# Raw weights to the place of their split parts, a third place for the chunks, x handed over by chunks of 128 tokens

## The chip, the cores and the metric
One core of one Trainium2 chip runs the whole kernel. It has five engines, each with an instruction queue that it works through in order: TensorE (PE, matmuls; PEld is its loading of weights), VectorE (DVE), ScalarE (ACT), GpSimd (POOL) and SyncE (SP), which here issues nearly all DMA transfers. The metric is the device time of one execution in microseconds.

## The reference
The input is four batches of 768 tokens with 8 heads of 48 elements. Three parts follow each other: a linear attention with a forget gate for each element, a layer of two matrices with a squared relu between them, and a soft mixture of experts.

```python
f = 1 / (1 + exp(-f_logit))
for t in range(S):                       # linear attention, per batch and head
    state = f[t][:, None] * state + outer(k[t], v[t])
    y[t] = q[t] @ state
x = y                                    # 3072 tokens x 384
h = maximum(x @ w_in, 0)                 # 384 -> 2048
x = (h * h) @ w_out                      # 2048 -> 384
logits = x @ phi                         # 32 slots: 8 experts, 4 slots each
d = softmax(logits, over tokens)
slot_out = per expert e: maximum((d.T @ x)[e] @ w1[e], 0) @ w2[e]
out = softmax(logits, over slots) @ slot_out
```

## The kernel before, in words
**Attention** runs in 24 chunks of 128 tokens, six to a batch. `chunk_load` (L129) brings a chunk's gate logits, k and q in one load `g<-fkq` (672 KB) into a place of pool g, and its v in another. `prep` (L145) works on them in place: exp of the logits (ACT L157), add 1 (DVE L161, on ACT for chunks 2 to 4), a running product along the tokens by four scans (DVE L163), a logarithm and an exp (ACT L170, L171), k times the product (DVE L172), and q times its inverse (DVE L178 to L180). The last of these, L180, is the last reader of the chunk's place. exp, add and scans are called the head of a chunk below. `knat`, `scores`, `state` and `values` do the matmuls; n is the transposed k copied out by ACT (L196). `values` writes minus y of a chunk into a tile y that holds a block of three chunks; after the third, six transfers (L269, L272) carry y of the whole block into x, the input of the layers (two of 216 KB, two of 48 and two of 24).

**The layers** run in 8 blocks of 384 tokens and 16 tiles of the inner dimension, 128 steps in all. A step (`layer1`, then `layer2`) has nine matmuls for `ph<-x,w`, on ACT a relu and two squares (`r` L347, `gh` L349, `r` L350), on DVE a subtraction (`gl<-r,gh`, L352), and nine matmuls for `o<-w,gh` and `o<-w,gl`. Each float32 product is done as three products of high and low parts, so x and w are split in two. The weights come as 64-bit floats: 16 raw tiles of 768 KB (`w_load`, L295, transfer L308), which `w_split` (L311) turns into a float32 `whi` with one ACT copy (L318), one ACT abs (L323) and three DVE instructions (L324, L325, L334), and `hl` (L114 on ACT, L115 on DVE) into a high and a low part in one of the 16 tiles of pool w. All 16 splits happen in the first 16 steps. The steps of blocks 0 and 1 are taken in turns (5, 9, 11 and 7 steps), from block 2 on block by block.

**Places.** Pool g has SLOTS = 4 places of 768 KB. Chunks 0, 1 and 2 take places 0, 1 and 2, and each later chunk takes places 0 and 1 in turn. Raw weights take places 2 and 3 in turn, each loaded one step ahead of its split. Two early loads of expert weights (`m2_load`, L516, transfer L527; in the steps 0 and 1 of block 3 in the order of the program) take places 2 and 3 after that, and when attention has ended, eight more loads take places 0 and 1 and six tiles of their own. In the last block's steps the loads go on into the 16 tiles of pool w as these come free, and what remains of the 32 loads stands at the end.

**The tail** (L536 on) runs the experts from these 32 tiles: `so<-m,ib` (L573) multiplies with the last of them; then the outputs.

**What sets the order.** The program is written as the loop of `fast_blocks`, with attention taken along by a table of targets. A scheduler then fixes the order of each engine's queue ahead of time, by its own model of times; on the chip an engine takes its queue in that order and waits where a semaphore isn't there yet. So where an instruction stands in a queue is fixed, and how long it waits is not.

Of the kernel before, what the change touches and what calls it, by code (L numbers as in the profile page):

```python
# [7 lines left out]
F32 = mybir.dt.float32  # L8
# [9 lines left out]
NP = H // 2  # L18
# [18 lines left out]
SLOTS = 4  # L37
PRE = 2
RAW = 6
AHEAD = 5  # L40
# [3 lines left out]
PREB = 3  # L44
# [14 lines left out]
class K:  # L59
# [70 lines left out]
    def chunk_load(self, i):  # L130
        nc, ap = self.nc, self.ap
        fkq = self.slot(i if i < 3 else (i + 1) % 2)[:DD].rearrange("d (x p t) -> d x p t", x=3, p=NP)
# [100 lines left out]
    def values(self, i):  # L233
# [18 lines left out]
        b, c = divmod(i, NC)  # L252
        if c == 0:
            self.y = ap.tile([DD, NP, TB], F32, tag="y", name="y", bufs=1)
        y = self.y
        t0 = c * C + before[0][0] * HC
        nc.scalar.mul(y[:, :, t0 : (c + 1) * C], pz[:, :, before[0][0] * HC :], -1.0)
        for j in range(2):
            o = y[:, :, c * C + j * HC : c * C + (j + 1) * HC]
            if U["S"][j] is None:  # L260
                nc.scalar.mul(o, py[j], -1.0)
            else:
                nc.vector.tensor_tensor(o, o, py[j], ALU.subtract)
        if c < NC - 1:
            return
        self.x_alloc(b)
        xl = self.x[b][1].bitcast(F32)
        for h in range(2):
            nc.sync.dma_start(out=xl[h * D : h * D + D], in_=y[h * HR : h * HR + D, :KT])  # L269
        for h in range(2):  # L270
            for e, n, kt, o in PLACE[6 + h]:
                nc.sync.dma_start(out=xl[o : o + n, kt], in_=y[h * HR + e : h * HR + e + n, KT])  # L272
# [26 lines left out]
    def w_load(self, ff):  # L299
        wide = self.A["w"].dtype != F32  # L300
        raw = self.slot(2 if ff > 1 and ff % 2 == 0 else 3)
# [9 lines left out]
    def w_split(self, ff, raw):  # L311

        nc, wr = self.nc, self.wr
        t = self.wp.tile([128, 2, 2 * DM], F32R, tag="w", name="w")
        if raw.dtype != F32:
# [3 lines left out]
            n = wr.tile([128, 2 * DM], I32, tag="whi", name="whi", bufs=2)  # L319
# [13 lines left out]
            raw = n.bitcast(F32)  # L333
            nc.vector.tensor_tensor(raw.bitcast(I32), n, lo, ALU.add)  # L334
        self.hl(t[:, 0], t[:, 1], raw)
# [181 lines left out]
    def m2_load(self):  # L517

        if self.loads < 32:
            j = self.loads % (SLOTS + RAW + NFF)  # L520
            if j < SLOTS:
                t = self.slot((j + 2) % SLOTS)
# [78 lines left out]
    def fast(self):  # L601
        with ExitStack() as main:
# [14 lines left out]
            raw = {0: self.w_load(0)}  # L617
# [4 lines left out]
    def fast_blocks(self, main, pst, ast, wst, raw):  # L622

        def stream():
            for i in range(2):
                yield from self.prep(i)
            for i in range(NCH):
# [3 lines left out]
                for j, n in enumerate((1, 1, 0, 0, 2) if ahead == 2 else (1, 1, 1, 0, 2)):  # L631
# [4 lines left out]
                    if j == (4 if i < 2 else 1) and i != 2 and new < NCH:  # L636
                        self.loaded[new] = self.chunk_load(new)
                    yield

# [39 lines left out]
        self.w_split(0, raw.pop(0))  # L679
# [219 lines left out]
```

## Time and profile before
| | us |
|---|---|
| median of three runs | 624.24 (623.1 to 625.67) |
| profiled execution, whole time | 626.73 |
| its span, first to last instruction | 624.9 |
| busy in it: PE, DVE, ACT | 585.5, 343.0, 335.5 |
| granted PE clock, mean | 0.986 of full speed |

The shares of the whole span (PE 94%, DVE 55%, ACT 54%) are an average of unlike stretches. In the first 41 us attention runs alone. Then the layers begin beside the rest of the splits of weights and attention at a high rate. From about 150 us layers and attention run side by side at a steady rate until 449 us, and then the layers alone until 573. The tail is last. What a microsecond is worth must be read in its own stretch, which the rows below allow.

### The profile page before, as it was taken

What the parts mean: (1) busy time and instruction counts of PE and PEld (TensorE: products, weight loads), DVE (VectorE), ACT (ScalarE), POOL (GpSimd) and SP (SyncE); (2) the same over time, 40 slices, a digit from 0 to 9 for tenths busy, and PEclk for the clock granted to TensorE, in tenths of its full rate; (3) what the DMA queues carried; (4) which work ended last, traced back from release to release, by engine and by line L of the source; (5) the groups of instructions that cost most, each with busy time, mean ns of one, the idle gap of its engine ahead of it and who ended that gap; (6) DMA issues with size and microseconds to landing.
All of it is one profiled execution on the core that took longest, in us unless ns stands there. A gap on an engine that the chain in (4) does not pass through costs nothing.

```text
span 624.9 us, 14327 instructions
## 1 busy us (share of the span) xinstructions
PE 585.5 (94%) x6065; PEld 525.3 (84%) x6065; DVE 343.0 (55%) x772; ACT 335.5 (54%) x697; POOL 4.0 (1%) x10
## 2 busy tenths in 40 slices
PE   3899989999999998999999999999999999999993
PEld 2777769899979897889989898989998999998352
DVE  5988899995445472555555455445333323223332
ACT  4657779985455553555454465554544545454121
POOL 0000000000000000000000000000000001000000
PEclk9998879999999999999999999999999999999998
DMA  9664655451122024021122103201300029576626
GB/s 241 179 189 155 202 167 172 162 200 55 32 64 58 3 58 96 1 59 58 35 63 59 42 17 97 58 2 65 102 1 2 1 87 355 204 251 252 257 105 252
DMA packets 18246, 69.62 MB, mean 111 GB/s; under 512 B 2832, under 2 KB 6928, under 8 KB 18176
## 3 DMA queue, kind: packets, MB, share of 16 engines
q1 hardware_dynamic: 18176, 68.64, 34.4%
q8 instruction: 49, 0.80, 0.5%
q14 instruction: 21, 0.17, 0.1%
HBM read 59.20 MB, written 4.72 MB: 102 GB/s over the span
## 4 chain that ended last, share of the span: by engine, by line
PE 71%; DMA 10%; ACT 8%; DVE 8%; issue 2%; SPq 0%; ACTq 0%; DVEq 0%
PE ph L119 10%; PE o L119 9%; PE ph L121 9%; DMA g<-fkq 9%; PE ph L120 9%; PE o L120 8%; PE o L121 8%; PE psm L244 3%; DVE ip L163 2%; PE psm L221 2%; PE so L573 2%; PE hp L551 2%; PE psm L206 1%; ACT gh L349 1%; PE psm L400 1%
## 5 line engine op out<-in xcount | busy, mean ns | idle before, releaser
L352 DVE TENSOR_TENSOR gl<-r,gh 128x384 fp32r<-128x384 f32 x128 | 71.2, 556 | 144.5 <-ACT r L350 144.4
L347 ACT ACTIVATE r<-ph 128x384 f32<-128x384 f32 x128 | 62.5, 489 | 148.0 <-PE ph L121 147.7
L119 PE MATMUL ph<-x,w 128*128 128x384 f32 x384 | 137.0, 357 | 2.5 <-ACT x L114 1.9
L120 PE MATMUL o<-w,gl 128*128 128x384 f32 x384 | 130.6, 340 | 4.8 <-DVE gl L352 4.7
L121 PE MATMUL ph<-x,w 128*128 128x384 f32 x384 | 131.8, 344 | 2.5 <-DVE x L115 2.5
L119 PE MATMUL o<-w,gh 128*128 128x384 f32 x384 | 130.5, 353 | 1.7 <-ACT gh L349 1.3
L120 PE MATMUL ph<-x,w 128*128 128x384 f32 x384 | 131.6, 343 | 0.2 <-DVE w L115 0.2
L121 PE MATMUL o<-w,gh 128*128 128x384 f32 x384 | 129.0, 336 | 0.0
L119 PEld LDWEIGHTS ph<-x,w 128*128 128x128 f32 x384 | 73.7, 192 | 9.9 <-issue 5.8
L120 PEld LDWEIGHTS o<-w,gl 128*128 128x128 f32 x384 | 72.4, 189 | 8.0 <-DVE gl L352 7.7
L121 PEld LDWEIGHTS ph<-x,w 128*128 128x128 f32 x384 | 73.9, 193 | 3.7 <-DVE x L115 3.6
L119 PEld LDWEIGHTS o<-w,gh 128*128 128x128 f32 x384 | 71.4, 189 | 6.6 <-ACT gh L349 2.6
L120 PEld LDWEIGHTS ph<-x,w 128*128 128x128 f32 x384 | 74.0, 193 | 0.4 <-DVE w L115 0.3
L121 PEld LDWEIGHTS o<-w,gh 128*128 128x128 f32 x384 | 72.4, 188 | 0.0
L349 ACT ACTIVATE gh<-r 128x384 fp32r<-128x384 f32 x128 | 67.1, 524 | 3.0
L350 ACT ACTIVATE r<-r 128x384 f32<-128x384 f32 x128 | 66.9, 523 | 2.8
L163 DVE TENSOR_TENSOR_SCAN ip<-g,ip,big 112x128 f32<-112x128 f32 x80 | 34.5, 468 | 0.3
L244 PEld LDWEIGHTS psm<-q,S 48*48 48x48 f32 (+1 forms) x704 | 25.9, 140 | 10.3 <-issue 5.7
L244 PE MATMUL psm<-q,S 48*48 48x64 f32 (+1 forms) x704 | 30.3, 235 | 4.0 <-DVE S L227 3.1
L180 DVE TENSOR_TENSOR q<-g,t 112x512 f32<-112x512 f32 (+1 forms) x25 | 16.5, 664 | 26.4 <-PE psm L244 26.4
L170 ACT ACTIVATE g<-ip 112x512 f32<-112x512 f32 (+1 forms) x25 | 15.3, 612 | 26.5 <-DVE ip L163 26.4
L161 DVE TENSOR_SCALAR g<-g 112x512 f32<-112x512 f32 (+1 forms) x22 | 8.9, 409 | 34.7 <-ACT g L157 34.7
(137 smaller groups left out, 662.0 us busy)
## 6 DMA issues: line engine op xcount, KB each, us to landing
m<-m SPq DMA_DIRECT2D x24, 768.0 KB, 4.4
g<-fkq SPq DMA_DIRECT2D x23, 672.0 KB, 5.2
g<-w SPq DMA_DIRECT2D x16, 768.0 KB, 4.6
g<-m SPq DMA_DIRECT2D x8, 768.0 KB, 4.9
v<-v SPq DMA_DIRECT2D x24, 192.0 KB, 4.5
out_dram<-ob SPq DMA_DIRECT2D x12, 384.0 KB, 3.6
x<-y SPq DMA_DIRECT2D x16, 216.0 KB, 5.2
x<-y SPq DMA_DIRECT2D x16, 48.0 KB, 3.9
```

The lines of the kernel that those rows point to most:

```text
L119: mm(out=out, lhsT=sh, rhs=mh, start=start, stop=False)
L120: mm(out=out, lhsT=sl, rhs=mh, start=False, stop=False)
L121: mm(out=out, lhsT=sh, rhs=ml, start=False, stop=stop)
L163: nc.vector.tensor_tensor_scan(ip[:, p], f[:, p], big, 1.0 if first else self.ip[:, p, C - 1 : C], ALU.mult, ALU.min)
L170: nc.scalar.activation(f[:, s], ip[:, s], AF.Ln)
L180: nc.vector.tensor_tensor(qt[:, s], q[:, s], t[:, s], ALU.mult)
L221: nc.tensor.matmul(out=pu[c][m, p], lhsT=U["n"][r, p, m], rhs=U["v"][r, hd * D : hd * D + D], start=True, stop=True)
L244: nc.tensor.matmul(out=pz[h * HR : h * HR + m, p, r], lhsT=U["S"][c][d, p * D : p * D + m], rhs=U["q"][d, p, r], start=True, stop=True)
L347: nc.scalar.activation(r, o, AF.Relu)
L349: nc.scalar.activation(gh, r, AF.Square)
L350: nc.scalar.activation(r, r, AF.Square)
L352: nc.vector.tensor_tensor(gl, r, gh.bitcast(F32), ALU.subtract)
```

## The change
Raw weights no longer use pool g. `w_load` takes a tile of pool w, where the split parts of the same size go later, and the first loads are issued at the start, up to WAHEAD = 4 tiles ahead of the split. `w_split` takes the tile for the parts only after the last reader of the raw tile (the add that makes `whi`). Pool g has three places now, and chunk i takes place i modulo 3. The tile y holds one chunk and has two buffers; each chunk's y goes to x by six transfers of a third of the size (72, 16 and 8 KB), and x is allocated at the first chunk of a block. The two early loads of expert weights are gone; nine are issued when attention has ended, and one more than before is left for the end. Line numbers of the changed kernel are lower by one to four here.

```diff
--- before.py
+++ after.py
@@ -34,14 +34,13 @@
 NE, FE = 8, 1024
 STEPS = 5
 LEAD = 4
-SLOTS = 4
-PRE = 2
+SLOTS = 3
 RAW = 6
+WAHEAD = 4
 AHEAD = 5
 FIRST = 18
 WARM = (1, 3, 1, 3)
 ONACT = 2, 3, 4
-PREB = 3
 PARTS = (2, 1)
 OT = 2

@@ -129,7 +128,7 @@

     def chunk_load(self, i):
         nc, ap = self.nc, self.ap
-        fkq = self.slot(i if i < 3 else (i + 1) % 2)[:DD].rearrange("d (x p t) -> d x p t", x=3, p=NP)
+        fkq = self.slot(i % SLOTS)[:DD].rearrange("d (x p t) -> d x p t", x=3, p=NP)
         if i == 0:
             nc.sync.dma_start(out=fkq[:, 0], in_=self.A["fkq"][i][:, 0])
             nc.sync.dma_start(out=fkq[:, 1:], in_=self.A["fkq"][i][:, 1:])
@@ -250,26 +249,23 @@
                     m = D if h else HR
                     nc.tensor.matmul(out=py[c][h * HR : h * HR + m, p], lhsT=U["v"][r, e : e + m], rhs=U["a"][r, h, p], start=True, stop=True)
         b, c = divmod(i, NC)
+        y = ap.tile([DD, NP, C], F32, tag="y", name="y", bufs=2)
+        t0 = before[0][0] * HC
+        nc.scalar.mul(y[:, :, t0:], pz[:, :, t0:], -1.0)
+        for j, r in enumerate(self.halves()):
+            if U["S"][j] is None:
+                nc.scalar.mul(y[:, :, r], py[j], -1.0)
+            else:
+                nc.vector.tensor_tensor(y[:, :, r], y[:, :, r], py[j], ALU.subtract)
         if c == 0:
-            self.y = ap.tile([DD, NP, TB], F32, tag="y", name="y", bufs=1)
-        y = self.y
-        t0 = c * C + before[0][0] * HC
-        nc.scalar.mul(y[:, :, t0 : (c + 1) * C], pz[:, :, before[0][0] * HC :], -1.0)
-        for j in range(2):
-            o = y[:, :, c * C + j * HC : c * C + (j + 1) * HC]
-            if U["S"][j] is None:
-                nc.scalar.mul(o, py[j], -1.0)
-            else:
-                nc.vector.tensor_tensor(o, o, py[j], ALU.subtract)
-        if c < NC - 1:
-            return
-        self.x_alloc(b)
+            self.x_alloc(b)
         xl = self.x[b][1].bitcast(F32)
+        ts = slice(c * C, (c + 1) * C)
         for h in range(2):
-            nc.sync.dma_start(out=xl[h * D : h * D + D], in_=y[h * HR : h * HR + D, :KT])
+            nc.sync.dma_start(out=xl[h * D : h * D + D, :, ts], in_=y[h * HR : h * HR + D, :KT])
         for h in range(2):
             for e, n, kt, o in PLACE[6 + h]:
-                nc.sync.dma_start(out=xl[o : o + n, kt], in_=y[h * HR + e : h * HR + e + n, KT])
+                nc.sync.dma_start(out=xl[o : o + n, kt, ts], in_=y[h * HR + e : h * HR + e + n, KT])

     def chunk(self, i):

@@ -297,8 +293,9 @@
         self.hl(xh[:, kt], xl[:, kt], xl[:, kt].bitcast(F32))

     def w_load(self, ff):
+
         wide = self.A["w"].dtype != F32
-        raw = self.slot(2 if ff > 1 and ff % 2 == 0 else 3)
+        raw = self.wp.tile([128, 4 * DM], F32, tag="w", name="raw")
         src = self.A["w"][ff]
         if wide:
             raw = raw.bitcast(I32).rearrange("p (w two) -> p w two", two=2)
@@ -311,12 +308,11 @@
     def w_split(self, ff, raw):

         nc, wr = self.nc, self.wr
-        t = self.wp.tile([128, 2, 2 * DM], F32R, tag="w", name="w")
+        n = wr.tile([128, 2 * DM], I32, tag="whi", name="whi", bufs=2)
         if raw.dtype != F32:

             lo, hi = raw[:, :, 0], raw[:, :, 1]
             nc.scalar.activation(lo, lo.bitcast(U32), AF.Copy, scale=2.0**-29)
-            n = wr.tile([128, 2 * DM], I32, tag="whi", name="whi", bufs=2)
             if not self.clamp:


@@ -330,9 +326,11 @@
                 nc.vector.tensor_scalar(n.bitcast(F32), n.bitcast(F32), LEAST, MOST, ALU.max, ALU.min)
                 nc.vector.tensor_scalar(n, n, 3, 0x3FFFFFFF, ALU.logical_shift_left, ALU.bitwise_and)
                 nc.vector.scalar_tensor_tensor(n, hi, -0x40000000, n, ALU.bitwise_and, ALU.bitwise_or)
-            raw = n.bitcast(F32)
-            nc.vector.tensor_tensor(raw.bitcast(I32), n, lo, ALU.add)
-        self.hl(t[:, 0], t[:, 1], raw)
+            nc.vector.tensor_tensor(n, n, lo, ALU.add)
+        else:
+            nc.vector.tensor_copy(n.bitcast(F32), raw)
+        t = self.wp.tile([128, 2, 2 * DM], F32R, tag="w", name="w")
+        self.hl(t[:, 0], t[:, 1], n.bitcast(F32))
         self.w.append(t)

     def layer1(self, b, ff):
@@ -519,7 +517,7 @@
         if self.loads < 32:
             j = self.loads % (SLOTS + RAW + NFF)
             if j < SLOTS:
-                t = self.slot((j + 2) % SLOTS)
+                t = self.slot(j)
             elif j < SLOTS + RAW:
                 t = self.tp.tile([128, 1536], F32, tag="m2", name="m2", bufs=RAW)
             else:
@@ -614,7 +612,7 @@
             self.consts2()
             for i in (1, 2):
                 self.loaded[i] = self.chunk_load(i)
-            raw = {0: self.w_load(0)}
+            raw = {ff: self.w_load(ff) for ff in range(2)}
             pst = fst.enter_context(ExitStack())
             self.fast_blocks(main, pst, ast, wst, raw)
             self.tail()
@@ -635,7 +633,13 @@
                     new = i + 3 if i < 2 else i + 2
                     if j == (4 if i < 2 else 1) and i != 2 and new < NCH:
                         self.loaded[new] = self.chunk_load(new)
+                        if new < 5:
+                            more_w()
                     yield
+
+        def more_w():
+            if len(raw) < NFF:
+                raw[len(raw)] = self.w_load(len(raw))

         st = stream()
         for _ in range(8):
@@ -676,8 +680,7 @@
         upto(FIRST)
         unsplit = 0
         split(0)
-        self.w_split(0, raw.pop(0))
-        raw[1] = self.w_load(1)
+        self.w_split(0, raw[0])
         wn = 1
         posts = iter(())
         pend = self.layer1(0, 0)
@@ -686,9 +689,9 @@
             if n == 3:
                 self.consts3()
             if wn < NFF:
-                if wn + 1 < NFF:
-                    raw[wn + 1] = self.w_load(wn + 1)
-                self.w_split(wn, raw.pop(wn))
+                while len(raw) < min(NFF, wn + WAHEAD):
+                    more_w()
+                self.w_split(wn, raw[wn])
                 wn += 1
                 if wn == NFF:
                     wst.close()
@@ -701,13 +704,11 @@
                     split(steps[n + 1][0])
                 nxt = self.layer1(*steps[n + 1])
             upto(target(n, b, ff))
-            if b == PREB and ff < PRE:
-                self.m2_load()
             if done == end and not self.tp:
                 ast.close()
                 self.tp = self.pool(main, "tp", side="right", reuse_waits="tile")
                 self.experts_begin(self.tp)
-                for _ in range(SLOTS - PRE + RAW):
+                for _ in range(SLOTS + RAW):
                     self.m2_load()
             self.layer2(b, ff, pend, begin, end_turn)
             pend = nxt
```

The order of three queues shows what moves. First DVE, around the steps 23 and 24. `L352` (after: `L350`) is gl of a step, `L172` (`L171`) makes k of a chunk, `L163` (`L162`) is a scan and `L161` (`L160`) the add, both of a chunk's head. Before:

```order
L209 TENSOR_TENSOR a<-psm,mask 128x256 x2
L352 TENSOR_TENSOR gl<-r,gh 128x384
L172 TENSOR_TENSOR k<-g,ip 112x512
L352 TENSOR_TENSOR gl<-r,gh 128x384 x2
L229 TENSOR_TENSOR S_100<-S_99,psm 112x192
L229 TENSOR_TENSOR S_97<-S_100,psm 112x192
L352 TENSOR_TENSOR gl<-r,gh 128x384
```

The same place in the changed kernel:

```order
L208 TENSOR_TENSOR a<-psm,mask 128x256 x2
L350 TENSOR_TENSOR gl<-r,gh 128x384
L171 TENSOR_TENSOR k<-g,ip 112x512
L177 TENSOR_TENSOR t<-ip,g 112x512
L160 TENSOR_SCALAR g<-g 112x512
L178 SCALAR_TENSOR_TENSOR t<-t,g 112x512
L162 SCALAR_TENSOR_TENSOR ip<-g,big 112x128 x4
L160 TENSOR_SCALAR g<-g 112x512
L162 SCALAR_TENSOR_TENSOR ip<-g,ip,big 112x128
L350 TENSOR_TENSOR gl<-r,gh 128x384
L162 SCALAR_TENSOR_TENSOR ip<-g,ip,big 112x128 x3
L350 TENSOR_TENSOR gl<-r,gh 128x384
```

The first gl of each piece is that of step 23, the next that of step 24. Two heads, of chunks 12 and 13, stand around step 24 now, the second of them a chunk further ahead than before.

ACT at the same place; `L347`, `L349`, `L350` are the relu and the two squares of a step (after: `L345`, `L347`, `L348`), `L157` (`L156`) is the exp that begins a chunk. Before, from the relu of step 22 on:

```order
L347 ACTIVATE r<-ph 128x384
L349 ACTIVATE gh<-r 128x384
L350 ACTIVATE r<-r 128x384
L157 ACTIVATE g<-g 112x512
L347 ACTIVATE r<-ph 128x384
L196 COPY n<-psm 128x448
L349 ACTIVATE gh<-r 128x384
L170 ACTIVATE g<-ip 112x512
L350 ACTIVATE r<-r 128x384
L171 ACTIVATE g<-g 112x512
L347 ACTIVATE r<-ph 128x384
```

The changed kernel, from the relu of step 23 on:

```order
L345 ACTIVATE r<-ph 128x384
L169 ACTIVATE g<-ip 112x512
L347 ACTIVATE gh<-r 128x384
L195 COPY n<-psm 128x448
L348 ACTIVATE r<-r 128x384
L170 ACTIVATE g<-g 112x512
L156 ACTIVATE g<-g 112x512 x2
L345 ACTIVATE r<-ph 128x384
L347 ACTIVATE gh<-r 128x384
L348 ACTIVATE r<-r 128x384
```

Where one exp stood between steps 22 and 23, two stand together between the squares of step 23 and the relu of step 24.

SP in the middle of the program, with the numbers of the tiles. `g_3604` holds chunk 16 before, `g_3670` chunk 16 after; v is a chunk's v. Before:

```order
L137 DMA g_3314<-fkq 112x1536
L139 DMA v_2793<-v 128x384
L137 DMA g_3604<-fkq 112x1536
L269 DMA x_2925<-y_2392 48x1152 x2
L272 DMA x_2925<-y_2392 32x384
L272 DMA x_2925<-y_2392 16x384
L272 DMA x_2925<-y_2392 32x384
L272 DMA x_2925<-y_2392 16x384
L139 DMA v_3058<-v 128x384
L137 DMA g_3879<-fkq 112x1536
```

The changed kernel:

```order
L138 DMA v_2552<-v 128x384
L136 DMA g_3670<-fkq 112x1536
L265 DMA x_2438<-y_2724 48x3x128 x2
L268 DMA x_2438<-y_2724 32x128
L268 DMA x_2438<-y_2724 16x128
L268 DMA x_2438<-y_2724 32x128
L268 DMA x_2438<-y_2724 16x128
L138 DMA v_2849<-v 128x384
L136 DMA g_3945<-fkq 112x1536
```

Behind every load of a chunk stand six transfers from y to x, each a third in size; before, they stood behind every third load.

## Rows read from the trace of the kernel before
**Rows 1.** Stretches: length, busy us of PE, PEld, DVE, ACT, POOL; clock, DMA, GB/s
```profile
90.00:150.00 60.00, 59.66 (x515) 56.92 (x515) 56.84 (x103) 52.24 (x102) 0.00 (x0) 1.00 0.51 167
...
150.00:520.00 370.00, 362.85 (x3832) 335.84 (x3831) 176.76 (x418) 189.44 (x406) 2.86 (x2) 1.00 0.18 49
...
573.00:625.00 52.00, 39.75 (x459) 22.02 (x457) 17.23 (x58) 10.98 (x30) 0.00 (x0) 0.96 0.55 213
```

**Rows 2.** Timeline of DVE, gl 8, 20, 23, 24: start, us, idle before
```profile
95.28 0.55 DVE L352 TENSOR_TENSOR gl<-r,gh 128x384 fp32r<-128x384 f32 x1
...
137.31 0.56 DVE L352 TENSOR_TENSOR gl<-r,gh 128x384 fp32r<-128x384 f32 x1
...
149.03 0.56 DVE L352 TENSOR_TENSOR gl<-r,gh 128x384 fp32r<-128x384 f32 x1 [0.46 <-ACT r L350]
...
151.79 0.56 DVE L352 TENSOR_TENSOR gl<-r,gh 128x384 fp32r<-128x384 f32 x1 [1.59 <-ACT r L350]
```

**Rows 3.** Waits of ACT, 150:520 (sum, times, longest); the longest in its timeline
```profile
ACT g L157 <- DMA g<-fkq: 13.7, 8, 4.4
...
248.60 0.63 ACT L157 ACTIVATE g<-g 112x512 f32<-112x512 f32 x1 [4.35 <-DMA g<-fkq]
```

**Rows 4.** Waits of PE, 150:520; its timeline behind five late chunk loads
```profile
PE o L120 <- DVE gl L352: 4.5, 4, 2.6
...
PE psm L400 <- ACT n L196: 1.3, 2, 1.0
...
PE psm L412 <- ACT n L196: 0.9, 1, 0.9
...
PE o L119 <- ACT gh L349: 0.2, 1, 0.2
...
176.12 0.64 PE L412 MATMUL psm<-th,ph 128*32 128x128 f32 x12 [0.93 <-ACT n L196]
...
250.29 0.44 PE L120 MATMUL o<-w,gl 128*128 128x384 f32 x1 [2.63 <-DVE gl L352]
...
387.49 0.44 PE L120 MATMUL o<-w,gl 128*128 128x384 f32 x1 [0.62 <-DVE gl L352]
...
273.47 0.55 PE L400 MATMUL psm<-ident,xf 128*128 128x128 f32 x3 [1.00 <-ACT n L196]
...
405.89 0.55 PE L400 MATMUL psm<-ident,xf 128*128 128x128 f32 x3 [0.27 <-ACT n L196]
```

**Rows 5.** Groups of instructions of DVE: busy us, mean ns, idle before
```profile
L163 DVE TENSOR_TENSOR_SCAN ip<-g,ip,big 112x128 f32<-112x128 f32 x80 | 34.5, 468 | 0.3
...
L172 DVE TENSOR_TENSOR k<-g,ip 112x512 f32<-112x512 f32 x23 | 15.7, 683 | 0.0
...
L178 DVE TENSOR_TENSOR t<-ip,g 112x512 f32<-112x512 f32 x23 | 15.8, 685 | 1.8 <-ACT g L171 1.8
...
L180 DVE TENSOR_TENSOR q<-g,t 112x512 f32<-112x512 f32 x23 | 15.8, 686 | 26.4 <-PE psm L244 26.4
...
L161 DVE TENSOR_SCALAR g<-g 112x512 f32<-112x512 f32 x20 | 8.3, 422 | 31.6 <-ACT g L157 31.6
```

**Rows 6.** Landing of chunk loads; x<-y transfers: KB, us to landing
```profile
DMA to landing us min/median/max: 4.2/5.2/11.1
...
x<-y SPq DMA_DIRECT2D x16, 216.0 KB, 5.2
...
x<-y SPq DMA_DIRECT2D x16, 24.0 KB, 3.4
```

**Rows 7.** Issues at L272: ns min/median/max, first and last start
```profile
L272 SPq DMA_DIRECT2D x<-y x32: 584/591/1612, 35.5 to 511.5; - x32
```

**Rows 8.** Tail: issue of late loads, a stretch, matmuls that read them
```profile
582.47 3.50 SPq L527 DMA_DIRECT2D g<-m  x4
...
588.00:594.00 6.00, 5.31 (x48) 1.70 (x48) 1.55 (x8) 0.59 (x1) 0.00 (x0) 1.00 1.01 421
...
602.09 1.46 PE L573 MATMUL so<-m,ib 128*32 128x256 f32 x25
```

More of the change, by code (lines that the diff above doesn't have):

```diff
@@ L765, in slow @@
                 self.wr = self.pool(st, "wr2")
-                self.gp = self.pool(st, "gp2")
+                raw = [self.w_load(ff) for ff in range(NFF)]
                 for ff in range(NFF):
-                    self.w_split(ff, self.w_load(ff))
+                    self.w_split(ff, raw[ff])
             self.fp = self.pool(main, "fp2")
```

## The prediction
> **What bounds the kernel now.** I read the table of busy time by stretch first: VectorE (DVE) is the fuller engine up to about 150 us (56.84 of 60.00 us in the stretch from 90), TensorE (PE) is at 362.85 of 370.00 us from there to 520, and in the last 52 us PE is idle for 12 [rows 1]. The reader is to see that a microsecond saved on a side engine counts only before 150 us or where PE visibly waits. Then the gl subtractions on DVE, one for each of the 128 steps of the layers: the idle time in front of them shows when DVE hands the lead over. In front of the 8th and the 20th there is none, in front of the 23rd 0.46 us and in front of the 24th 1.59 us, ended by ScalarE (ACT) both times [rows 2]. So DVE could have done the 24th at 151.79 − 1.59 = 150.2 us, and from there PE sets the pace. Third, the waits in the long middle stretch: ACT waits 13.7 us in 8 places for a load of a chunk [rows 3], and PE, behind it, waits 6.9 us in all, for gl, n and gh [rows 4]. Last, the loads around 580 us and the matmuls that read them.
>
> The profiled execution took 626.73 us with a span of 624.9, so 1.83 us lie around the span. The median of the runs shown is 624.24, 2.49 lower; I take my sum off 626.73 and then 2.49.
>
> **Early part: raw weights ahead, third place.** Raw weights no longer sit in chunk places 2 and 3, and the chunks take three places in turn. Both change DVE's queue. I counted instructions ahead of each gl in the two orders and gave each the mean of its form. Up to the 20th gl there are 13 fewer: six scans at 468 ns, two L172 at 683, one each of L178, L179 and L180 at about 685 [rows 5], and two tiny ones of the range test that I leave at nothing: 2.81 + 1.37 + 2.06 = 6.2 us. Means ignore overlap. From the 8th gl to the 23rd the sum grows by 57.3 us and the trace by 149.03 − 95.28 = 53.75 us [rows 2], a factor of 0.938. So DVE is 6.2 × 0.938 = 5.9 us early at step 20.
>
> That lead doesn't last. With a third place, the head of a chunk (exp, add, four scans) can be queued one chunk sooner, and the order puts it there: behind the 23rd gl of the changed order stand an add, four scans, another add and another scan before the 24th. Up to the 24th gl, DVE now has two instructions more than before, an L161 and a scan, 422 + 468 = 0.9 us [rows 5], 0.85 with the factor. Until the 23rd it still had 7 fewer (3.7 us). DVE could then do the 24th gl at 150.2 + 0.85 = 151.05, against 151.79 before: **−0.7 us**. What hides the rest is PE: once DVE is no longer last, steps run at PE's rate, and PE's own instructions are the same in number. The earlier raw loads save nothing beyond that; what DVE did with the idle of ACT's first split was attention's work, and that is in the count.
>
> Bounds: −5.9 if the lead survives. Above: two exps, of chunks 12 and 13, now stand together in ACT's queue ahead of the 24th relu (the order of ACT), and the second waits for a load; behind it wait the relu, both squares and gl, and for these PE. The nearest row is the longest wait of ACT for a chunk, 4.35 us, which cost PE 2.63 [rows 3, 4]; at full price 4.35 − 0.7 gives +3.7. I take −0.7, since by my count the place of chunk 13 comes free some 8 us before that exp and a load lands in 5.2 us at the median (11.1 at most) [rows 6].
>
> **Middle part: waits for chunks.** The obvious reading is that a third place takes the 13.7 us off ACT. I don't take it. In both orders the exp stands two relus behind the step whose q frees its place: before, chunk 14's exp behind relu 36, now chunk 15's behind the same relu, and so on at 41, 46, 52, 57, 62, 68, 73 and 78. The load is one chunk further ahead, and its exp too: the distance in time from issue to use is as it was. One such place fewer exists at the end, the load at 399, worth 0.27 us of PE [rows 4].
>
> What does change is what rides behind these loads. Before, the 11 loads of this stretch are of two kinds. Four stand at the end of a block, with x<-y of the whole block right behind (216 KB twice, then the small pieces); they cost PE 0.93 + 0.21, 2.63 + 0.64, 0.62 and 0.62 = 5.65 us, 1.41 each. Seven have nothing but v behind them; they cost 1.00 and 0.27 = 1.27 us, 0.18 each [rows 4] (shown are the first and last of each kind, and the longest). Now every load has a third of those bytes (192 of 576 KB) behind it: by thirds 0.18 + (1.41 − 0.18) / 3 = 0.59 us. Ten loads: 5.9, against 6.9: **−1.0 us**. Bounds: all ten at 0.18 gives 1.8, which is −5.1; all ten at the price of a block end gives 14.1, which is +7.2. By bytes the third is nearer, so the interpolation stands; by number of transfers (six behind every load, as six before) the upper end would be.
>
> The landing times speak for some of both: a transfer of 216 KB lands in 5.2 us, one of 24 KB still in 3.4 [rows 6]. The Trainium skill (Perfetto Trace Analysis, DMA Optimizations) says that transfers under 2 KB carry a significant overhead each, so that batching pays, and also that splitting lets a piece start sooner where the DMA engines are idle. By the first rule the sum would go to the upper end, 14.1 us of PE waits (rival C); by the second it stays as I took it. The trace agrees with the first on the time that a small transfer takes to land; how long it holds up a load beside it, no row shows.
>
> SP has 96 more transfers to issue (144 against 48) at 0.59 us [rows 7], 56 us in all, spread over some 480; what hides them is that the next chunk's load stands ahead of each group (the order of SP) and the one after it is due some 20 us later, so I cost them at nothing. If that cover went, 6 × 0.59 = 3.5 us would be late for v, which attention's matmuls read a chunk later. Having y by chunk removes a wait of ACT for the single y and costs the same copies: nothing.
>
> **Tail.** Two early loads of expert weights go and one place more is not there, so seven are left for the end instead of six. The six are issued from 582.47 on (the row has four of them), and the queues move 421 GB/s then [rows 8]. A load is 128 × 1536 × 4 bytes = 786 KB, so 1.87 us of transfer: six from 582.47 on are through at 593.7, seven at 595.6. The last matmuls that read such weights begin at 602.09 [rows 8], 6.5 us later. **0**; without that cover +1.9.
>
> **Sum.** 626.73 − 0.7 − 1.0 = 625.0, and less 2.49: **622.5 us**. Its own range is 619.5 to 626.5: early −0.7 with up to 3 either way, middle −1.0 with 2 either way.
>
> **Rivals.**
> A, the third place does its work: loads land a chunk ahead of their exps and the 6.9 us go. 624.24 − 6.9 − 0.7 = 616.6. For it: the places are one more and ACT's wait is the longest entry after PE's in the middle. Against it: the order, in which the exps move up with the loads.
> B, the early lead of 5.9 us is kept, because the pulled-up heads cost DVE less than their means there, lying beside work that waits anyway: 624.24 − 5.9 − 1.0 = 617.3. For it: DVE is the bound until 149 and the head of a later chunk is pure advance. Against it: gl is strictly behind them in DVE's queue, and the 24th is where the count turns.
> C, slower: six transfers stand behind every load, and a transfer in the same queues holds up the load whatever its size. Then ten loads cost 1.41 each: 624.24 + 7.2 − 0.7 = 630.7. It decides from the point at which a load lands later than about 5 us after its issue. For it: the block ends of before, and 3.4 us for 24 KB. Against it: the 5.65 us have 3.27 from one block end alone, so the price of the other three is 0.8.
>
> **How the numbers follow.** Forecast 0.55, A 0.10, B 0.13, C 0.14; 0.08 is for slips on either side. The range from 616.5 to 629.0 takes in A and B and the early stall of ACT (3.7 for −0.7 gives 626.9), and leaves out C. A measurement of this kernel tells 0.5%, 3.1 us, from no change. Below 621.1 is faster: A, B, and a small part of the forecast's range, 0.30. Above 627.4 is slower: C and the worst of the ACT stall, 0.17. Between them 0.53.
>
> **What would show it.** In the profile of the changed kernel: the 20th gl at about 131.4 and the 24th between 150 and 152 us (B: the 24th at 146). ACT's waits for chunks at the same steps as before with 10 to 14 us in sum (A: under 3), and PE's waits for gl and n at 5 to 7 us (C: 12 or more). The last late load through by 599 us. The prediction is wrong if the change in the span comes from elsewhere: from PE's clock in the first 90 us, from PE waiting for x, or from the last 52 us.

## The result, and the profile after

The changed kernel takes 618.22 us (median of 4 runs, 617.23 to 619.29) against 624.95 before (4 runs): a ratio of 0.9897, 95% interval 0.9867 to 0.9926. The forecast was 622.5. The profiled execution takes 618.22 us with a span of 616.4.

The two spans can be cut so that PE does exactly the same instructions in each piece: up to the start of the 29th gl (1651 records of matmuls), from there to the 89th (2694), to the 128th (1260), and the rest. First before, then after; columns as in [rows 1].

```profile
0.00:168.95 168.95, 149.05 (x1651) 134.96 (x1652) 140.16 (x276) 117.98 (x226) 1.10 (x8) 0.96 0.52 159
168.95:427.97 259.02, 251.87 (x2694) 230.29 (x2694) 138.21 (x331) 135.00 (x293) 0.00 (x0) 1.00 0.19 52
427.97:571.73 143.76, 143.76 (x1260) 137.24 (x1259) 46.87 (x109) 71.50 (x149) 2.86 (x2) 1.00 0.36 125
571.73:624.90 53.17, 40.81 (x464) 22.76 (x462) 17.78 (x59) 10.98 (x30) 0.00 (x0) 0.96 0.55 210
```

```profile
0.00:164.34 164.34, 146.65 (x1651) 131.44 (x1652) 141.43 (x281) 119.12 (x229) 1.86 (x9) 1.00 0.53 161
164.34:417.67 253.33, 249.94 (x2694) 230.37 (x2694) 137.27 (x327) 133.59 (x290) 0.00 (x0) 1.00 0.19 53
417.67:561.44 143.77, 143.77 (x1260) 137.26 (x1259) 47.07 (x109) 71.50 (x149) 2.03 (x1) 1.00 0.37 124
561.44:616.40 54.96, 42.50 (x464) 23.09 (x462) 17.79 (x59) 10.99 (x30) 0.00 (x0) 0.93 0.58 220
```

The differences are −4.6, −5.7, 0 and +1.8 us, −8.5 in all. In the first piece PE is busy 2.4 us less for the same work (granted clock 1.00 in place of 0.96) and idle 2.2 us less. In the second it is idle 3.39 us in place of 7.15. The last piece got longer. The medians differ by 6.7 us: before's profiled execution (626.73) is 1.8 us above its median, the changed kernel's (618.22) is at its own.

DVE's rows that answer to [rows 2], the 8th, 20th, 23rd and 24th gl:

```profile
87.34 0.56 DVE L350 TENSOR_TENSOR gl<-r,gh 128x384 fp32r<-128x384 f32 x1
...
129.66 0.56 DVE L350 TENSOR_TENSOR gl<-r,gh 128x384 fp32r<-128x384 f32 x1
...
142.85 0.56 DVE L350 TENSOR_TENSOR gl<-r,gh 128x384 fp32r<-128x384 f32 x1 [1.09 <-ACT r L348]
...
147.59 0.53 DVE L350 TENSOR_TENSOR gl<-r,gh 128x384 fp32r<-128x384 f32 x1
```

The lead over before is 7.9, 7.7, 6.2 and 4.2 us: it shrinks at the 24th, as forecast, but is far from gone. The waits that answer to [rows 3, 4], from 164 to 418 us:

```profile
ACT g L156 <- DMA g<-fkq: 7.7, 7, 2.2
```

```profile
PE psm L398 <- ACT n L195: 1.8, 2, 1.5
PE o L119 <- DVE gl L350: 1.3, 3, 0.5
PE psm L410 <- ACT n L195: 0.3, 1, 0.3
```

### The profile page after: what moved, and what is told of

It is laid out like the page before. It is cut to its first block, busy times and chain, and to the rows that moved or that the text cites. A ratio compares the mean times of both kernels' runs of the same rounds, so it can differ in the third digit from the quotient of the medians.

```text
span 616.4 us, 14476 instructions
## 1 busy us (share of the span) xinstructions
PE 582.9 (95%) x6065; PEld 522.2 (85%) x6065; DVE 343.6 (56%) x772; ACT 335.2 (54%) x697; POOL 3.9 (1%) x10
## 2 busy tenths in 40 slices
DMA packets 27465, 69.65 MB, mean 113 GB/s; under 512 B 4368, under 2 KB 16912, under 8 KB 27392
## 4 chain that ended last, share of the span: by engine, by line
PE 74%; DVE 8%; DMA 8%; ACT 5%; SPq 2%; issue 2%; DVEq 0%; ACTq 0%
PE o L118 10%; PE ph L118 9%; PE o L119 9%; PE ph L120 9%; PE ph L119 9%; PE o L120 9%; DMA raw<-w 4%; PE psm L243 3%; DVE ip L162 2%; DMA g<-fkq 2%; PE hp L549 2%; PE psm L220 2%; PE so L571 2%; PE psm L205 2%; PE psm L250 1%
## 5 line engine op out<-in xcount | busy, mean ns | idle before, releaser
L350 DVE TENSOR_TENSOR gl<-r,gh 128x384 fp32r<-128x384 f32 x128 | 71.3, 557 | 145.4 <-ACT r L348 143.2
L345 ACT ACTIVATE r<-ph 128x384 f32<-128x384 f32 x128 | 62.5, 488 | 141.1 <-PE ph L120 141.1
L118 PE MATMUL ph<-x,w 128*128 128x384 f32 x384 | 134.7, 351 | 0.9 <-ACT x L113 0.9
L119 PE MATMUL ph<-x,w 128*128 128x384 f32 x384 | 129.4, 337 | 0.0
L120 PE MATMUL ph<-x,w 128*128 128x384 f32 x384 | 129.0, 337 | 0.0
L118 PEld LDWEIGHTS ph<-x,w 128*128 128x128 f32 x384 | 72.3, 188 | 8.4 <-issue 5.8
L119 PEld LDWEIGHTS ph<-x,w 128*128 128x128 f32 x384 | 72.4, 189 | 0.2
L120 PEld LDWEIGHTS ph<-x,w 128*128 128x128 f32 x384 | 72.2, 188 | 0.1
L347 ACT ACTIVATE gh<-r 128x384 fp32r<-128x384 f32 x128 | 67.1, 524 | 5.1 <-PE o L120 2.3
L348 ACT ACTIVATE r<-r 128x384 f32<-128x384 f32 x128 | 66.9, 523 | 2.7
L162 DVE TENSOR_TENSOR_SCAN ip<-g,ip,big 112x128 f32<-112x128 f32 x80 | 33.3, 468 | 0.6 <-ACT g L158 0.2
L205 PEld LDWEIGHTS psm<-q,k 48*64 48x64 f32 x768 | 18.2, 148 | 8.8 <-ACT n L195 3.0
```

The costliest lines, as they stand in the source:

```text
L118: mm(out=out, lhsT=sh, rhs=mh, start=start, stop=False)
L119: mm(out=out, lhsT=sl, rhs=mh, start=False, stop=False)
L120: mm(out=out, lhsT=sh, rhs=ml, start=False, stop=stop)
L162: nc.vector.tensor_tensor_scan(ip[:, p], f[:, p], big, 1.0 if first else self.ip[:, p, C - 1 : C], ALU.mult, ALU.min)
L205: nc.tensor.matmul(out=pa[h][r, p], lhsT=U["k"][d, p, r], rhs=U["q"][d, p, r], start=True, stop=True)
L345: nc.scalar.activation(r, o, AF.Relu)
```

## The experiments

All were timed against the kernel before on the chip of their own group (medians 623.88, 622.33 and 623.21 there), so ratios are compared. Profile rows are the piece to the 29th gl and the piece from there to the 89th, with the columns above. Theory 1 at the start: raw weights ahead give the early gain, x by chunk the middle gain. Theory 2: the third place gives both.

**e1, raw weights alone** (from the changed kernel: two places in turn, and the old end of `values`, with y and its six transfers by block).

```diff
-        fkq = self.slot(i % SLOTS)[:DD].rearrange("d (x p t) -> d x p t", x=3, p=NP)
+        fkq = self.slot(i if i < 3 else (i + 1) % 2)[:DD].rearrange("d (x p t) -> d x p t", x=3, p=NP)
...
-        y = ap.tile([DD, NP, C], F32, tag="y", name="y", bufs=2)
+        if c == 0:
+            self.y = ap.tile([DD, NP, TB], F32, tag="y", name="y", bufs=1)
...
```

> The changed kernel with two parts undone: chunks in two places in turn as before, y and x<-y by whole blocks as before. What is left is the raw weights in the pool of their parts, up to four ahead (and the two early expert loads gone). Theory 1 (raw weights ahead give the early gain of 4.6 us, x<-y by chunk gives the middle gain of 5.7 us): step 29 about 4.6 us earlier than before, steps 29 to 89 as long as before (259 us), 620 to 622 us in all. Theory 2 (the third place gives both): step 29 as before, 624 to 626 us.

Measured: 624.05 us, ratio 1.0013 (0.9991 to 1.0034).

```profile
0.00:166.45 166.45, 146.33 (x1651) 132.00 (x1652) 139.87 (x275) 117.84 (x226) 1.10 (x8) 0.99 0.49 157
166.45:423.55 257.10, 251.81 (x2694) 230.31 (x2694) 138.33 (x332) 135.04 (x293) 0.00 (x0) 1.00 0.19 52
```

**e2, x by chunk alone** (the kernel before with the new end of `values`).

> The kernel before with one part of the change: y by chunk and six transfers of a third of the size for each chunk; four places, raw weights in two of them, chunks in two in turn. Theory 1: step 29 as before (169 us), steps 29 to 89 take 253 to 254 us in place of 259, 619 to 620 us in all. Theory 2: all as before, 624 to 626 us. My forecast's own rule (small pieces behind all loads, 0.59 us of PE each) would give 624.

Measured: 619.85 us, ratio 0.9936 (0.9915 to 0.9957).

```profile
0.00:166.85 166.85, 149.81 (x1651) 133.72 (x1652) 140.06 (x275) 117.56 (x226) 1.85 (x9) 0.99 0.53 164
166.85:419.66 252.81, 250.05 (x2694) 230.17 (x2694) 137.97 (x332) 135.37 (x293) 0.00 (x0) 1.00 0.20 53
```

**e3, two places** (the changed kernel with the line of `chunk_load` as before).

> The changed kernel with one part undone: chunks 3 and later take places 0 and 1 in turn, the third place is used by chunk 2 alone. Theory 1: 618 us, as the changed kernel, with step 29 at 164 us and 253 us from step 29 to 89. Theory 2: 624 to 626 us, with step 29 at 169 us and 259 us from there.

Measured: 614.98 us, ratio 0.9886 (0.9847 to 0.9925).

```profile
0.00:163.01 163.01, 145.76 (x1651) 131.13 (x1652) 140.07 (x276) 117.57 (x226) 1.85 (x9) 1.00 0.52 163
163.01:416.91 253.90, 250.37 (x2694) 230.19 (x2694) 137.96 (x331) 135.22 (x293) 0.00 (x0) 1.00 0.20 52
...
560.68:613.90 53.22, 40.81 (x464) 22.77 (x462) 17.80 (x59) 10.99 (x30) 0.00 (x0) 0.95 0.60 227
```

**e4, y by block** (the changed kernel with the old end of `values`).

> The changed kernel with one part undone: y and x<-y by whole blocks as before; raw weights ahead and three places stay. Theory 1: the middle gain is lost: step 29 at 164 us, steps 29 to 89 take 259 us, 623 to 624 us in all. Theory 2: 618 us with 253 us from step 29 to 89.

Measured: 620.53 us, ratio 0.9964 (0.9930 to 0.9997).

```profile
0.00:165.45 165.45, 145.25 (x1651) 132.16 (x1652) 141.01 (x281) 118.75 (x229) 1.10 (x8) 0.99 0.50 157
165.45:422.80 257.35, 252.57 (x2694) 232.00 (x2694) 137.15 (x326) 134.59 (x290) 0.00 (x0) 0.99 0.20 53
```

The reader is to see the middle piece: 257.1 and 257.4 us with x by block, in two places and in three, and 252.8, 253.3 and 253.9 with x by chunk. Theory 2 falls by e3, which has the whole gain without the third place. Theory 1 holds for the middle in its sign. Its size is less sure, for two of the three profiles with x by block hold one late load of a chunk at the same step. In before the load issued at 240.19 us landed after 8.3 us and held ACT for 4.35 [rows 3]; in e1 the load of that step held ACT for 1.92; in e4 it held ACT for 3.45, PE waited 1.73 us for the gl behind it, and then the granted clock fell to 0.77 over 5 us. ACT's row and that stretch, both of e4:

```profile
244.87 0.63 ACT L156 ACTIVATE g<-g 112x512 f32<-112x512 f32 x1 [3.45 <-DMA g<-fkq]
```

```profile
245.00:250.00 5.00, 3.44 (x13) 3.45 (x14) 3.59 (x8) 3.88 (x9) 0.00 (x0) 0.77 0.04 15
```

From the 45th gl to the 49th before takes 19.20 us, e4 18.96, e1 16.76, the changed kernel 15.85. With the excess over e1 taken off, 2.4 and 2.2 us, the middle is 256.6 in before and 255.2 in e4. So x by chunk is worth 3.2 to 4.3 us with two places (e1 against e3 and e2) and 1.3 to 1.8 with three (e4 so corrected against e8 below and the changed kernel), and what the late load costs where it comes. No profile with x by chunk has a wait of ACT for a chunk over 2.2 us in this piece.

The early half of theory 1 misses: e1 was to reach the 29th gl 4.6 us earlier and take 620 to 622 us, and is 2.5 earlier and by its median no faster; e2 was to be no earlier, and is 2.1 earlier. Beside x by chunk raw weights gain another 0.5% (0.9936 to 0.9886, intervals that just touch). With y by block the third place takes 0.5% off by the medians (e1 to e4, again intervals that touch). The two profiles put 1.0 us of it ahead of the 29th gl and 1.75 us in the last stretch (54.98 and 53.23), where the place can't be the reason, since the changed kernel has three places and 54.96; e4's late load hides some 2 us in the middle.

**e5, thirds at the block's end** (the kernel before; three y tiles, and e2's six transfers for each of them behind the third chunk).

```diff
+        self.ys = [y] if c == 0 else self.ys + [y]
+        if c < NC - 1:
+            return
+        self.x_alloc(b)
+        for c, y in enumerate(self.ys):
...
```

> The kernel before, with y in three tiles of a chunk and eighteen transfers of a third of the size, all issued at the end of the block, where six stood. Theory P (what cost the middle was a block's 576 KB piled behind one chunk load): nothing is gained over before, steps 29 to 89 take 257 to 260 us, 623 to 625 us in all. Theory S (pieces in themselves move quicker or hold a load less): steps 29 to 89 take 253 us as with x by chunk, and about 620 us. If small transfers carry a cost of their own, slower than before: 262 us or more in the middle.

Measured: 621.87 us, ratio 0.9998 (0.9971 to 1.0025). The median is that of theory P; the middle piece lies between the two, 2.0 us below e1's.

```profile
168.11:423.20 255.09, 250.16 (x2694) 230.10 (x2694) 137.92 (x331) 135.28 (x293) 0.00 (x0) 1.00 0.20 53
```

**e6, x sent twice** (the changed kernel, its six transfers once into x and once into a tile `no`).

```diff
+        no = self.fp.tile([128, KT, C], F32, tag="no", name="no", bufs=1)
+        for to in (xl[:, :, ts], no):
...
```

> The changed kernel, with each chunk's six transfers from y issued twice, the second time into a tile that nothing reads (192 KB and six issues more behind every chunk load). By the price of my forecast, 0.41 us for each third, some eleven loads make 4.5 us more: 258 us from step 29 to 89, 622 to 623 us in all. If a third more costs nothing, 253 us there and 618 us in all. If what gains in the middle is that x comes earlier and not that less stands behind a load, also 253 us.

Measured: 631.73 us, ratio 1.0142 (1.0105 to 1.0179).

```profile
0.00:179.55 179.55, 147.41 (x1651) 132.60 (x1652) 142.98 (x280) 118.36 (x229) 1.86 (x9) 0.97 0.51 156
179.55:431.61 252.06, 249.98 (x2694) 230.30 (x2694) 137.35 (x326) 133.52 (x290) 0.00 (x0) 1.00 0.23 62
```

In the middle, twice the transfers and bytes behind every chunk load cost nothing: 252.1 us. So up to twelve transfers and 384 KB behind a load neither bytes nor number had a price; the interpolation of my forecast, and rival C, are gone. A block's 576 KB behind one load, as in before and e4, is not tested by it. The loss, 11 to 15 us at the 29th gl against the two profiles of the changed kernel, is early, where ACT waits for the copies themselves before it can write y again. The row is from ACT's waits up to 180 us; the rest of the loss was not traced, and the twelve issues of SP for each chunk are a guess for it.

```profile
ACT y L254 <- DMA no<-y: 6.1, 1, 6.1
```

e5 completes it: thirds sent late gain nothing in the median. By that, smaller transfers do not pay by themselves.

**e7, raw weights one ahead** (two places; `WAHEAD = 2`, only raw 0 at the start, no loads in the stream).

> The two-places kernel with raw weights loaded one tile ahead of their split, as before, but still into the pool of the split parts. If the early gain of the raw weights (2.5 us at step 29, 4 us beside x by chunk) comes from the distance, it goes: the 2nd gl at 58 us, step 29 at 166 to 167 us, 618 to 619 us in all. If it comes from the places (four tiles to write to and no wait for a place), it stays: step 29 at 163 us, 615 us in all.

Measured: 618.17 us, ratio 0.9935 (0.9915 to 0.9956), the same as e2 with raw weights in the old places. The 2nd gl starts at 61.25 us, in e3 at 50.37.

```profile
0.00:166.23 166.23, 148.02 (x1651) 133.12 (x1652) 139.54 (x275) 118.40 (x226) 1.86 (x9) 0.99 0.50 160
166.23:419.85 253.62, 249.52 (x2694) 230.21 (x2694) 137.98 (x331) 135.35 (x293) 0.00 (x0) 1.00 0.19 52
```

So the part of the raw weights goes with the distance, not with the pool, as far as two intervals that just touch (0.9915 to 0.9956 and e3's 0.9847 to 0.9925) can say it.

**e8, the changed kernel again.**

> The changed kernel again, beside the others on one chip. 618 us; the last stretch, from the last gl to the end, 53.2 us if the 1.8 us more in its first profile was a fall of the clock by chance, 55.0 us if the seventh late load of expert weights causes it.

Measured: 617.09 us, ratio 0.9920 (0.9887 to 0.9954).

```profile
0.00:168.17 168.17, 150.08 (x1651) 134.11 (x1652) 141.49 (x280) 119.05 (x229) 1.86 (x9) 0.95 0.51 157
168.17:422.00 253.83, 250.38 (x2694) 230.30 (x2694) 137.23 (x327) 133.59 (x290) 0.00 (x0) 1.00 0.19 53
565.75:620.70 54.95, 42.50 (x464) 23.03 (x462) 17.80 (x59) 10.98 (x30) 0.00 (x0) 0.93 0.57 219
```

The same kernel is 3.8 us later at the 29th gl than in its first profile, and PE is busy 3.4 us longer up to there: its clock stood at 0.54 from 35 to 49 us in this execution. That execution took 622.46 us, 5.4 above the median of the twelve; the two of them with a mean clock of 0.98 took 621.7 and 622.5, the nine with 0.995 or more 614.0 to 620.2, and the one between them 623.2. One profile alone doesn't settle a few us of the early part. The last stretch is the one that was expected if the seventh load causes it; e3 and e4, with seven as well, speak against that.

**e9 and e10, ACT's order at three block ends** (e2 with a one-column tile that makes the first cast of x wait; the diff is e9's, e10 has 13 in place of 14).

```diff
+        if not self.clamp and (b, ff) in [(2, 14), (3, 14), (4, 14)]:
+            nc.scalar.mul(self.tick, r[:, :1], 0.0)
-        self.hl(xh[:, kt], xl[:, kt], xl[:, kt].bitcast(F32))
+        if b in (3, 4, 5):
+            self.nc.scalar.activation(xh[:, kt], xl[:, kt].bitcast(F32), AF.Identity, bias=self.tick)
...
```

In the kernel before, ACT's logarithm of a chunk (L170), which waits for the scans behind a late exp, stands between the relu and the squares of steps 47, 63 and 79. With x by chunk and two places (e2, e3) the order has casts of x there and the logarithm behind the squares; e5 has that order too. The changed kernel has another one: casts at these steps, and the logarithm between the relu and the squares of the next step (48, 64 and 80), where it waits 1.24, 1.47 and 0.77 us.

> The kernel before with x by chunk, and with the first cast of x at three block ends made to wait for the squares of steps 47, 63 and 79 (through a one-column tile that ACT writes there and that the cast adds as zero). That puts ACT's logarithm of a chunk, which waits for DVE's scans, ahead of the squares of those steps again, as in the kernel before; the transfers stay small and early. Theory O (the middle gain is one of order: what stands behind a late chunk load on ACT): 2 to 3 us of the gain go, steps 29 to 89 take about 255.4 us against 253 in the next kernel, 621 to 622 us in all. Theory T (the gain is the transfers' own): 253 us as in the next kernel.

> Control of the kernel ahead: the same extra instructions, but the casts wait for the squares of steps 46, 62 and 78, which leaves ACT's order as it is with x by chunk (two casts, then the squares, then the logarithm). Both theories: 253 us from step 29 to 89, 619 to 620 us in all.

Measured: 621.79 us, ratio 0.9989 (0.9963 to 1.0015), and 619.85 us, ratio 0.9944 (0.9919 to 0.9968). The middle piece, e9 first:

```profile
165.23:419.58 254.35, 250.41 (x2694) 230.18 (x2694) 138.79 (x331) 136.53 (x296) 0.00 (x0) 1.00 0.19 52
```

```profile
167.63:421.07 253.44, 250.06 (x2694) 230.16 (x2694) 138.02 (x332) 136.92 (x296) 0.00 (x0) 1.00 0.19 52
```

The medians lose what theory O expected (2 to 3 us, 0.45%), the profiles only 0.9 us in the stretch meant. But e9's profile is of the one of its twelve executions that took least (618.39), so it can't show what the median lost. Taken by the medians, early thirds without e2's order gain nothing (e9, 0.9989), e2's order without early thirds gains nothing (e5, 0.9998), and both together do (e2 and e10, 0.9936 and 0.9944). The casts of x come later in e9 too, so the place of the logarithm isn't tested by itself; and the changed kernel, whose logarithm again stands ahead of squares, has nearly as short a middle as e2. How the gain divides between that order, shorter waits for loads and the first block end, where the order was left, stays open.

**e11, raw weights eight ahead** (e3 with `WAHEAD = 8`).

> The two-places kernel with raw weights up to eight tiles ahead in place of four. If distance is what counts in the early part, some of the rest goes: step 29 before 163 us, 613 to 615 us in all. If four are enough, the five loads in a row stand ahead of chunk loads and x on the queues: the 2nd gl stands behind 87 rows of DVE in place of 72, step 29 at 164 to 166 us, 616 to 618 us in all.

Measured: 623.94 us, ratio 0.9997 (0.9968 to 1.0027): the whole gain is lost, and more than either view had expected.

```profile
0.00:175.20 175.20, 153.13 (x1651) 138.82 (x1652) 141.54 (x275) 118.55 (x226) 1.86 (x9) 0.95 0.48 151
```

Five loads of 768 KB stand in a row there, and the 8th gl starts at 102.25 us, in e3 at 86.61. This profile is of an execution 3.9 us above its median, with a clock of 0.95 in the piece (e3: 1.00). Four ahead is better than eight, and by the medians better than one (e7), with intervals that just touch.

**e12, two places again.**

> The two-places kernel again, to be set against the changed kernel: 615 to 617 us. If the third place costs something, this one is 1 us or more below the changed kernel's 617 to 618 in this ratio too (0.989 or less of before); if not, the ratios overlap at 0.990 to 0.992.

Measured: 616.08 us, ratio 0.9882 (0.9840 to 0.9925).

```profile
0.00:162.78 162.78, 145.79 (x1651) 131.19 (x1652) 139.98 (x275) 117.34 (x226) 1.86 (x9) 1.00 0.52 163
```

With e3's 0.9886 it lies below the changed kernel's 0.9897 and 0.9920, but all four intervals overlap. The third place gains nothing beside the other two parts, and may cost some tenths of a per cent. Two places are the best version seen, not shown better than the change.

## Why the prediction was right or wrong

**Sign and reach.** It said no change or slightly faster, 622.5, and 616.5 to 629.0 with the rivals. The time is 618.2, below the forecast's own range of 619.5 to 626.5 and near rival B's 617.3; by the prediction's own bound of 621.1 it is faster, which it had given 0.30. That it lies between 616.5 and 629.0 is owed to the room left for A and B, and is luck in part, for neither is what happened. Right were the sign, the weak third place and the tail's loads. Two terms were too small, and all three signs of being wrong that the prediction had named came in part: PE's clock in the first 90 us, PE's waits for x, and a change in the last 52 us. The clock, from 45 to 90 us, before and then after:

```profile
45.00:90.00 45.00, 39.65 (x424) 32.36 (x423) 40.13 (x74) 32.86 (x63) 0.00 (x0) 0.85 0.54 169
```

```profile
45.00:90.00 45.00, 40.49 (x428) 34.33 (x425) 41.85 (x76) 36.73 (x70) 0.00 (x0) 1.00 0.77 228
```

**Early, −0.7 forecast, −4.6 in the profile.** The failed step is "DVE could then do the 24th gl at 151.05": it did it at 147.59. The lead at the 20th was 7.7 us where the count gave 5.9. From the 20th to the 24th the changed queue took 17.9 us (129.66 to 147.59); before took 12.9 (137.31 to 150.2), so the pulled-up heads cost 5.0 where the count gave 6.75 (5.9 and 0.85). That part holds: e8 takes 17.9 us there too. The lead does not: in e8 the 20th gl is at 133.49 and the 24th at 151.42, inside the forecast's 150 to 152, but in an execution with the lower clock:

```profile
133.49 0.56 DVE L350 TENSOR_TENSOR gl<-r,gh 128x384 fp32r<-128x384 f32 x1
...
151.42 0.53 DVE L350 TENSOR_TENSOR gl<-r,gh 128x384 fp32r<-128x384 f32 x1
```

Scans in a row overlap, which a count at a form's mean leaves out: in the changed kernel four of them take 1.36 and 1.60 us between the 20th and the 24th gl, where the mean gives 1.87. The larger error is the view behind it, that only DVE counts before 150 us. The row cited for it has PE busy for 59.66 of the 60.00 us, more than DVE's 56.84 [rows 1], and PE waits for inputs in the early part:

```profile
PE ph L121 <- DVE x L115: 2.5, 1, 2.5
PE ph L119 <- ACT x L114: 1.9, 2, 1.3
PE ph L119 <- ACT w L114: 0.6, 1, 0.6
PE ph L120 <- DVE w L115: 0.2, 1, 0.2
```

These are before's waits for x and w, 5.2 us; after has one line of the kind, 0.9 us:

```profile
PE ph L118 <- ACT x L113: 0.9, 2, 0.6
```

I had costed earlier x and earlier raw weights at nothing. Both together take 5.9 us off the 29th gl (e3) and 6.2 in a second profile (e12). Alone they take 2.5 (e1) and 2.1 (e2), less than the 3.8 us between the two profiles of the changed kernel. Where the time goes differs: in e2 PE is idle for 17.0 us up to there in place of before's 19.9, in e1 it is idle as long (20.1) and busy 2.7 us less. In e3 it is idle for 17.3 us and busy 3.3 us less (149.05 to 145.76) at a clock of 1.00 in place of 0.96; e8 shows the price of that clock in the other direction. Why the clock is higher in one kernel or execution than in another stays open.

**Middle, −1.0 forecast, −5.7 in the profile.** Right in the outcome: beside x by chunk the third place gives PE nothing (253.90 us in e3 without it, 253.33 and 253.83 with it). Not in the reason, that the distance from issue to use is as it was: ACT's waits for chunks fall from 10.9 us in e3 to 7.7 and 8.1, below the 10 to 14 that the prediction named (over ten chunks in place of eleven), but PE's idle time, 3.5 us in e3 and 3.4 and 3.5 with the place, does not follow. Wrong: the price by bytes. The step "by thirds 0.18 + (1.41 − 0.18) / 3" took for a price of bytes what stood at the block's end: x late, the logarithm ahead of the squares, and one load of 8.3 us, which alone made 3.27 of the 5.65. I had named that load against rival C and still used it in the mean. Twice the bytes cost nothing (e6). PE's waits for gl and n came to 3.4 us where 5 to 7 had been named. Of the two rules weighed there, the one on splitting is what the medians bear out, where ACT's order can use the early pieces (the Trainium skill, Perfetto Trace Analysis, DMA Optimizations): 0.9936 when each third leaves as it is ready (e2), 0.9998 when the thirds leave together (e5), 0.9989 when they leave early and the casts wait (e9). The one on small transfers shows no price in the middle, though the packets under 2 KB went from 6928 to 16912; no transfer of x is that small as a whole. Doubled (e6), the transfers cost 11 us or more early, where the copies hold y.

**Tail, 0 forecast, +1.8 in the profile.** The matmuls that read late loads did not wait. What got longer is the first group of expert matmuls, before and after:

```profile
581.36 2.76 PE L551 MATMUL hp<-g,ia 128*32 128x512 f32 x18 [0.30 <-DVE ia L509]
```

```profile
571.05 4.46 PE L549 MATMUL hp<-g,ia 128*32 128x512 f32 x18 [0.30 <-DVE ia L507]
```

The granted clock is 0.64 from 570 to 574 us, so mostly the lower of its two levels (1.2 of 2.4 GHz), and 1.00 in the same place before. e3 and e12, with the same seven late loads, have 53.22 us in the tail and e4 53.23, so the seventh load does not cause it by itself. But of nine profiles with seven late loads six show a tail of 54 us or more, of the five with six late loads none. What lowers the clock there stays open.

**SP at nothing.** True for the change: its 96 more issues show in no wait of PE in the middle. Doubled (e6), they were no longer free in the early part. The cover that I named, 20 us between loads, holds only from 150 us on; in e3 loads of chunks are issued at 47.90 and 56.20 us.

**Rivals.** A falls beside x by chunk (e3 has the gain without the place), while its amount came close by another way; with y by block the place may be worth 0.5% (e1 and e4). B, the lead kept, holds for 4.6 of its 5.9 us in the first profile and for 0.8 in e8's. C falls with e6.

## What to carry to other kernels

Hand a result on when it is ready, not when its block is full: by the medians here, early pieces and an order of the consumer's queue that can use them gained together, and neither alone; smaller transfers by themselves gained nothing. Cut two traces where the bottleneck engine has done the same instructions; the pieces then differ only by its idle time and its clock, and a stretch in which two engines are both nearly full has to be priced for both. Before interpolating between a few events, take out the one that makes up most of their sum, and look what else is special about their place; do the same for every profile that is set against it (e4 had such a load as well). Before a few us are read from one profile, see where its execution stands among the timed ones: e9's took the least time of twelve, e8's and e11's the second most.

## What the runs showed of the hardware that was not expected

The same kernel had PE at a granted clock of 0.54 over 14 us of the early part in one execution (e8) and at 1.00 in another, with 3.4 us more PE time for the same instructions up to the 29th gl; 0.54 is close to the lower of its two levels (1.2 of 2.4 GHz). From 34 to 36 us, just before it fell, PE was busy for 1.41 us there and for 2.00 in the other. In the tail, 18 matmuls of `hp` took 2.76 us at the full clock and 4.46 us where it had fallen, with the same instructions in front of them. Twelve small transfers behind a chunk load of 672 KB, 384 KB in all, did not delay it: ACT's waits for chunk loads in the middle were 7.2 us with them (e6) and 7.7 with six (the changed kernel), and the piece with the doubled transfers was the shortest of all, 252.06 us.
